# A window on the transfers in flight, a third Q/K buffer and a new plan for the attention stage

## Chip, cores, metric

One core of one Trainium2 chip. The metric is device time in microseconds of one execution.

## The reference

Sparse causal attention with a linear bias, then two blocks on its output. B = 2, H = 8, S = 768, D = 64, model width 512. All inputs are float32 but the weights, which arrive as float64.

```
scores = q @ k.T / sqrt(D) - slope[h] * dist          # keep: the last 96 keys, and the first 8
x = concat_heads(softmax(scores) @ v)                 # B x S x 512
u = x + ((x.T @ U @ V).T)                             # rank 32 over the sequence
x = u + relu(u @ w_ch1) @ w_ch2                       # 512 -> 2048 -> 512
xk, xr = mixes of x with x shifted by one row (mu_k, mu_r)
out = sigmoid(xr @ w_r) * (relu(xk @ w_k)**2 @ w_v)   # 512 -> 1024 -> 512
```

## The kernel before, in words

Attention goes by eight pairs of heads (`PRS`: two batches, four pairs each) and, in a pair, by six tiles of 128 queries. A tile's scores are products of `QS` with a window of 256 gathered columns of `KK` (`s_mm`, L446). VectorE adds the bias and takes the row minimum out of PSUM (`s_min`, L454), ScalarE takes exponentials (`s_exp`, L462), VectorE inverts the sums of three tiles (L467, L468), GpSimd scales (`s_norm`, L474). TensorE transposes the tile (`tp`, L481), ScalarE or VectorE copies it out (`PT`, L705 or L707), and TensorE multiplies with V (`p_first` L496, `p_rest` L507: "PV" here) into `xa` and `xb`, which go to `yp`.

Beside it, in the same stretch, run the constants `UV` and the first weight slices: a float64 tile of 512 KB comes in through the staging buffer `stg` (L687, three tiles; UV at L724) and is turned into a high and a low part by ScalarE (L641, L653), VectorE (L636, L645, L649) and GpSimd (L657): "a conversion". When the four pairs of the first batch are done, its rank-32 product follows: transposes `xtp` (L755) with evictions `xt`, `gps` (L773), the sums `gsum` and `uv` (L779 to L794), `hps` (L804) added to `yp` (L809), the split `us` (L840, L843), and 48 matmuls of the first slice of w_ch1, `aps` (L874). Then, from the transposes of the second batch on, the program is written out by hand: alternating blocks of 48 `aps` and 48 `bps` matmuls, then `kps`, `prs`, `pvs`.

What sets the order of all this up to the second batch's transposes is a planner, `Flow`. Every step (a few instructions) has a kind; `COST` gives the engine, how long it is held and how late its result is; `rank` plus `BIAS` order the steps that could start within `SLACK` of each other; `caps` hold the number of tiles of each pool. `Flow.run` picks a step, advances the engines' times and emits its instructions, so the order on every queue is fixed when the program is built. Loads are steps on SP (SyncE's queue, which issues the transfers in order): `dq` (Q, 384 KB), `dk` (K or V, 768 KB), `ds` (a staging tile, counted as 512 KB), `dm` (the constants `mu`). A load that needs a buffer stands behind the last step that reads the old tile. The pools: Q and K two tiles each (`qkp`), V two, P ten, PT eight.

The first pair's Q and K and the second's are issued before the planner begins. In SyncE's queue stands also the load of `flag_i` (L1117), which GpSimd computes; it decides whether a general path (not taken here) is run.

## Time and profile before

| | |
|---|---|
| median of 3 runs | 525.47 us (525.38 to 527.12) |
| the profiled execution's own time | 525.22 us |
| its span, first to last instruction | 523.4 us |
| TensorE busy | 503.3 us, 96% of the span |
| VectorE, ScalarE, GpSimd busy | 305.3, 217.0, 184.7 us |
| transfers on the hardware queue of SyncE | 46.28 MB in 13,248 packets |

The durations in the text are from the profiled execution. PE is TensorE's matmul, PEld its weight load, DVE is VectorE, ACT is ScalarE, POOL is GpSimd, SP is SyncE. A time in brackets behind a row is the idle time of the engine before it, with the instruction that ended it.

### The profile page before, as it was taken

The numbers are of one execution on the slowest core, as the hardware profiler recorded it, in microseconds if no ns is written. First come the engines' busy times: TensorE is split into PE (matmuls) and PEld (weight loads), VectorE is DVE, ScalarE is ACT, GpSimd is POOL, SyncE is SP. The second block draws the span as 40 slices with busy tenths as digits, with TensorE's granted clock in tenths as the row PEclk, the third lists the DMA queues.
The fourth block names the chain that finished last, engine by engine and source line by source line (L and its number), as shares of the span: only waits on it lengthen the run. The fifth ranks groups of instructions, "written<-read, shape, count | busy, mean of one in ns | idle before, by whom it ended". The sixth has DMA issues, their size and how long they took to land.

```text
span 523.4 us, 8648 instructions
## 1 busy us (share of the span) xinstructions
PE 503.3 (96%) x3314; PEld 411.2 (79%) x3314; DVE 305.3 (58%) x673; ACT 217.0 (41%) x507; POOL 184.7 (35%) x247
## 2 busy tenths in 40 slices
PE   7788999999999999999999999999999999999994
PEld 4577677778888888888888888887888888888884
DVE  6898997789983746528365837796043522352110
ACT  6798987535430503204032312444912441144100
POOL 7685786026400404004040403635712442144100
PEclk9999999999999999999999999999999999999998
DMA  8977542323451310403104310031001000100010
GB/s 316 352 285 264 199 153 83 121 81 106 150 194 34 103 58 10 152 0 111 51 13 149 122 40 0 20 142 41 0 21 40 22 0 21 41 20 1 21 41 27
DMA packets 13587, 47.19 MB, mean 90 GB/s; under 512 B 1760, under 2 KB 2144, under 8 KB 13536
## 3 DMA queue, kind: packets, MB, share of 16 engines
q1 hardware_dynamic: 13248, 46.28, 25.7%
q8 instruction: 28, 0.46, 0.3%
q10 hardware_dynamic: 288, 0.26, 0.2%
q14 instruction: 23, 0.19, 0.1%
HBM read 43.39 MB, written 3.15 MB: 89 GB/s over the span
## 4 chain that ended last, share of the span: by engine, by line
PE 79%; DVE 11%; DMA 4%; ACT 2%; issue 2%; POOL 0%; SPq 0%; DVEq 0%; ACTq 0%
PE aps L874 24%; PE bps L896 21%; PE pvs L1081 13%; PE kps L1051 10%; PE prs L1070 6%; DMA KK<-in_k_dram 3%; DVE cvc L645 2%; DVE P L454 2%; DVE cvc L649 2%; PE s L446 2%; DVE PT L707 1%; DMA stg<-in_wv_dram 1%; PE tp L481 1%; ACT P L462 1%; DVE yp L900 1%
## 5 line engine op out<-in xcount | busy, mean ns | idle before, releaser
L874 PE MATMUL aps<-us,w1s 128*128 128x512 f32 x576 | 133.5, 390 | 0.0
L896 PE MATMUL bps<-rs,w2s 128*128 128x512 f32 x576 | 132.5, 389 | 0.0
L896 PEld LDWEIGHTS bps<-rs,w2s 128*128 128x128 f32 x576 | 108.0, 188 | 23.3 <-PE gps L773 0.8
L874 PEld LDWEIGHTS aps<-us,w1s 128*128 128x128 f32 x576 | 107.8, 188 | 22.6 <-issue 0.4
L878 ACT ACTIVATE rs<-aps 128x512 fp32r<-128x512 f32 x48 | 28.2, 595 | 94.6 <-PE aps L874 94.5
L1051 PE MATMUL kps<-mix,wk 128*128 128x512 f32 x288 | 66.1, 389 | 0.5 <-ACT kf L1055 0.5
L1051 PEld LDWEIGHTS kps<-mix,wk 128*128 128x128 f32 x288 | 54.0, 188 | 12.1 <-ACT kf L1055 0.9
L1081 PE MATMUL pvs<-wv,kh 128*128 128x512 f32 (+1 forms) x208 | 61.9, 373 | 0.0
L882 DVE SCALAR_TENSOR_TENSOR rs<-aps,rs 128x512 fp32r<-128x512 f32 x48 | 32.7, 686 | 42.0 <-ACT rs L878 42.0
L645 DVE SCALAR_TENSOR_TENSOR cvc<-cvc,cvt 128x512 uint32<-128x512 uint32 (+1 forms) x53 | 50.8, 960 | 7.5 <-ACT cvc L641 6.2
L641 ACT ACTIVATE cvc<-stg 128x512 f32<-128x512 f32 (+1 forms) x53 | 35.1, 675 | 44.1 <-DMA stg<-in_w_dram 18.8
L900 DVE TENSOR_TENSOR yp<-bps,yp 128x512 f32<-128x512 f32 (+1 forms) x64 | 33.9, 550 | 25.7 <-PE bps L896 25.7
L474 POOL TENSOR_SCALAR P<-P,sm 128x192 f32<-128x192 f32 x96 | 43.4, 473 | 14.4 <-DVE sm L468 5.8
L1033 POOL TENSOR_SCALAR mixt<-yp,mu 128x512 f32<-128x512 f32 (+1 forms) x32 | 21.6, 681 | 74.2 <-DVE mixf L1035 29.6
L649 DVE SCALAR_TENSOR_TENSOR cvc<-stg,cvc 128x512 uint32<-128x512 uint32 x52 | 45.1, 874 | 0.6
L657 POOL TENSOR_TENSOR w2s<-cvc,w2s 128x512 fp32r<-128x512 f32 x16 | 23.2, 1466 | 62.9 <-ACT w2s L653 59.7
L657 POOL TENSOR_TENSOR w1s<-cvc,w1s 128x512 fp32r<-128x512 f32 x16 | 23.3, 1472 | 60.3 <-ACT w1s L653 59.7
L462 ACT ACTIVATE P<-P,nm 128x192 f32<-128x192 f32 x96 | 42.5, 448 | 3.0 <-DVE nm L454 2.7
L1081 PEld LDWEIGHTS pvs<-wv,kh 128*128 128x128 f32 x208 | 38.1, 188 | 6.9
L1061 POOL TENSOR_TENSOR kl<-kf,kh 128x512 fp32r<-128x512 f32 x24 | 31.0, 1292 | 30.6 <-ACT kh L1060 30.6
L1081 PE MATMUL pvs<-wv,kl 128*128 128x512 f32 (+1 forms) x104 | 38.8, 373 | 0.0
L1035 DVE SCALAR_TENSOR_TENSOR mixf<-yp,mu,mixt 128x512 f32<-128x512 f32 (+1 forms) x32 | 20.3, 653 | 29.8 <-POOL mixt L1033 29.7
(113 smaller groups left out, 586.9 us busy)
## 6 DMA issues: line engine op xcount, KB each, us to landing
stg<-in_w_dram SPq DMA_DIRECT2D x32, 512.0 KB, 4.0
vin<-in_v_dram SPq DMA_DIRECT2D x8, 768.0 KB, 5.2
KK<-in_k_dram SPq DMA_DIRECT2D x7, 768.0 KB, 7.2
stg<-in_wk_dram SPq DMA_DIRECT2D x8, 512.0 KB, 4.2
stg<-in_wv_dram SPq DMA_DIRECT2D x8, 512.0 KB, 3.6
out_dram<-sg SPq DMA_DIRECT2D x11, 256.0 KB, 2.0
QS<-in_q_dram SPq DMA_DIRECT2D x7, 384.0 KB, 5.6
stg<-in_wr_dram SPq DMA_DIRECT2D x4, 512.0 KB, 3.6
```

Source lines behind the costliest of these rows:

```text
L462: nc.scalar.activation(out=Px, in_=Px, func=ACTF.Exp, scale=-1.0, bias=z["nm"][:, i, x:x + 1], accum_out=z["sm"][:, i, x:x + 1])
L474: engine.tensor_scalar(out=Px, in0=Px, scalar1=z["sm"][:, i, x:x + 1], scalar2=1.0, op0=ALU.mult, op1=ALU.mult)
L641: nc.scalar.activation(out=z["c"].bitcast(F32), in_=parts(z)[1].bitcast(F32), func=ACTF.Copy, scale=2.0 ** -112)
L645: nc.vector.scalar_tensor_tensor(out=z["c"], in0=z["c"], scalar=3, in1=z["t"], op0=ALU.logical_shift_left, op1=ALU.bitwise_or)
L649: nc.vector.scalar_tensor_tensor(out=z["c"] if plain is None else plain, in0=parts(z)[1], scalar=0x80000000, in1=z["c"], op0=ALU.bitwise_a ...
L657: engine.tensor_tensor(out=lo, in0=z["c"].bitcast(F32), in1=hi.bitcast(F32), op=ALU.subtract)
L874: nc.tensor.matmul(rs[g, c, f], lhsT=wsl(("w1", g), lw, kk, f * 128, 128), rhs=us[c][:, lx, kk, :], start=(kk == 0 and n == 0), stop=(kk = ...
L882: nc.vector.scalar_tensor_tensor(out=r[:, 1, f, :], in0=rs[g, c, f], scalar=0.0, in1=r[:, 0, f, :].bitcast(F32), op0=ALU.max, op1=ALU.subt ...
L896: nc.tensor.matmul(ps, lhsT=wsl(("w2", g), lw, f, o * 128, 128), rhs=r[:, lx, f, :], start=(n == 0), stop=(n == 11))
L900: nc.vector.tensor_tensor(out=ys, in0=ps[:, a:e], in1=ys, op=ALU.add)
L1051: nc.tensor.matmul(ps, lhsT=wsl("wk", lw, kk, f * 128, 128), rhs=xk[:, lx, kk, :], start=(n == 0), stop=(n == 11))
L1081: nc.tensor.matmul(pv, lhsT=ks[c][lx][:, f, t * 128:(t + 1) * 128], rhs=wsl("wv", lw, f, c0, c1 - c0), start=(n == 0), stop=(n == 23))
```

## The change

- `Flow` keeps the list of transfers sent. `before(x)` goes back from transfer x and adds the planner's sizes until they pass `LIMIT`, 2,000 KB; the transfer found there must have landed before x is issued. The plan takes its end as a lower bound for x, and `link` writes the wait into the program (a dependency between the two transfers).
- Pools: Q and K three tiles each, P twelve, PT ten. The room comes from the descriptor scratch, which goes from its default to 1,024 bytes.
- V loads have a kind of their own (`dv`). `BIAS`, `SLACK`, `RATE`, `LAND` and the ranks of the conversions have other values, so that the planner comes to another order. The load functions return their instruction.

```diff
-        ... "ch": [("PE", 0.68, 0.95)], ...
+        ... "ch": [("PE", 0.68, 0.95, 0.15)], ...
-        "dq": [("SP", 0.45, 384.0)], "dk": [("SP", 0.45, 768.0)], "ds": [("SP", 0.45, 512.0)], "dm": [("SP", 0.45, 4.0)],
+        "dq": [("SP", 0.45, 384.0)], "dk": [("SP", 0.45, 768.0)], "dv": [("SP", 0.45, 768.0)], "ds": [("SP", 0.45, 512.0)], "dm": [("SP", 0.45, 4.0)],
-    BIAS = {"ch": -9, "vd": -36, "ttr": -1.5, "xt": -26, "y": 8, "hm": -14, "vps": -8, "ga": 11, "tp": 17, "pt": 1.1,
-            "exp": -21, "sm": -6}
+    BIAS = {"dv": 8, "va": -5, "pt": 2.3, "vps": -3, "vd": -14}
-    SWITCH, SLACK, RATE, LAND = 0.13, 0.06, 390.0, 2.1
+    SWITCH, SLACK, RATE, LAND, LIMIT = 0.13, 0.02, 380.0, 2.4, 2000
...
+    def before(self, x):
+        n = self.COST[x.kind][0][2]
+        for a in reversed(self.sent):
+            n += self.COST[a.kind][0][2]
+            if n > self.LIMIT:
+                return a
+        return None
...
+            first = self.before(x) if eng == "SP" else None
+            if first is not None:
+                go = max(go, first.end)
...
-            x.fn(eng) if len(self.COST[x.kind]) > 1 else x.fn()
+            x.ins = x.fn(eng) if len(self.COST[x.kind]) > 1 else x.fn()
+            if eng == "SP":
+                first = self.before(x)
+                if first is not None:
+                    self.link(x.ins, first.ins)
+                self.sent.append(x)
...
-            pt_p = pool("ptp", 8, "right", cctx)
+            pt_p = pool("ptp", 10, "right", cctx)
-            np_p = pool("npp", 10, "right", cctx)
+            np_p = pool("npp", 12, "right", cctx)
-            qk_p = pool("qkp", 2, "right", bctx)
+            qk_p = pool("qkp", 3, "right", bctx)
...
-                fl = Flow({"a": 4, "t": 4, "P": 10, "PT": 8, "q": 2, "k": 2, "v": 2, ...},
-                          {"PE": 5.9, "ACT": 6.6, "DVE": 6.4, "POOL": 10.0, "SP": 3.1}, 7.6)
+                fl = Flow({"a": 4, "t": 4, "P": 12, "PT": 10, "q": 3, "k": 3, "v": 2, ...},
+                          {"PE": 5.9, "ACT": 6.6, "DVE": 6.4, "POOL": 10.0, "SP": 3.1}, 10.0,
+                          lambda a, b: tc.add_manual_dep(a.ins, b.ins.name, mybir.DependencyInfo(
+                              mybir.DependencyClass.Sync, mybir.DependencyReason.DATA), reason="transfers"))
...
-                        def conversion(r, behind=None, shift=0):
+                        def conversion(r, behind=None, shift=0, early=0):
-                            ds = fl.add("ds", lambda: z.update(stage(src)), new=[toks["st"]], rank=r - 12, behind=[behind])
+                            ds = fl.add("ds", lambda: z.update(stage(src)) or z["dma"], new=[toks["st"]], rank=r - 12 + early, behind=[behind])
-                        uvd = conversion(24, lks[0])
-                        w1d = [conversion(r, lk, x) for r, lk, x in zip((34, 44, 54, 64), lks[1:], (-24, 0, 14, 9))]
+                        uvd = conversion(24, lks[0], 0, 0)
+                        w1d = [conversion(r, lk, *x) for r, lk, x in zip((34, 44, 54, 64), lks[1:], ((0, 0), (-1, 11),
+                                                                                       (0, -19), (18, 0)))]
                         for r in (84, 86, 88, 90):
-                            conversion(r)
+                            conversion(r, None, -5, 0)
...
-    nc = _bacc.Bacc("TRN2", target_bir_lowering=False, num_devices=1)
+    nc = _bacc.Bacc("TRN2", target_bir_lowering=False, num_devices=1, dynamic_dma_scratch_size=1024)
```

What this does to the order shows best in three places. In the changed program lines lie 17 to 20 lower down. SyncE's queue, from V of the first pair on (`QS`, `KK` and `vin` are tiles of Q, K and V, `stg` staging tiles; the numbers are tile numbers). Before:

```order
L342 DMA vin_211<-in_v_dram 128x1536
L219 DMA mu_59<-in_mu_dram 128x8
L687 DMA stg_214<-in_w2_dram 128x512
L687 DMA stg_216<-in_w2_dram 128x512
L687 DMA stg_218<-in_w2_dram 128x512
L1117 TENSOR_LOAD flag_i_62
L331 DMA QS_279<-in_q_dram 128x768
L337 DMA KK_289<-in_k_dram 128x1536
L342 DMA vin_293<-in_v_dram 128x1536
L331 DMA QS_352<-in_q_dram 128x768
L337 DMA KK_363<-in_k_dram 128x1536
```

Now:

```order
L359 DMA vin_211<-in_v_dram 128x1536
L348 DMA QS_213<-in_q_dram 128x768
L354 DMA KK_215<-in_k_dram 128x1536
L236 DMA mu_59<-in_mu_dram 128x8
L743 DMA stg_330<-in_UV_dram 128x384
L1137 TENSOR_LOAD flag_i_62
L348 DMA QS_352<-in_q_dram 128x768
L359 DMA vin_393<-in_v_dram 128x1536
L354 DMA KK_414<-in_k_dram 128x1536
L348 DMA QS_442<-in_q_dram 128x768
L706 DMA stg_505<-in_w1_dram 128x512
```

Q and K of the third pair (`QS_213`, `KK_215`) have moved ahead of the flag; the three w2 tiles are gone from here and UV has come forward.

ScalarE's queue where the rank-32 product of the first batch goes on after its transposes (`xt` evicted transposes, `P,sm` exponentials, `gsum` and `uv` the sums). Before, from the third instruction behind the last `xt` on:

```order
L705 COPY PT<-tp 128x384
L462 ACTIVATE P,sm<-P,nm 128x192 x6
L641 ACTIVATE cvc<-stg 128x512
L462 ACTIVATE P,sm<-P,nm 128x192 x5
L779 COPY gsum<-gps 32x512
L462 ACTIVATE P,sm<-P,nm 128x192
L653 CAST w1s<-cvc 128x512
```

Now:

```order
L724 COPY xt<-xtp 128x512 x5
L724 COPY PT<-tp 128x384
L479 ACTIVATE P,sm<-P,nm 128x192 x5
L798 COPY gsum<-gps 32x512
L672 CAST w1s<-cvc 128x512
L479 ACTIVATE P,sm<-P,nm 128x192 x3
```

Between the last `xt` and `gsum` there were 15 instructions (two exponentials and the four rows above `gsum`), and there are 6 now.

TensorE's queue at the end of the attention stage (`tp` transposes of P; the PV rows are left out). Before:

```order
L446 MATMUL s<-KK,QS 64x192 x8
L804 MATMUL hps<-uv 128x256 x2
L874 MATMUL aps<-us,w1s 128x512 x36
L481 MATMUL tp<-ident,P 128x128 x18
L755 MATMUL xtp<-ident,yp 128x128 x24
L773 MATMUL gps<-xt,uvf 32x512 x6
L896 MATMUL bps<-rs,w2s 128x512 x48
```

Now:

```order
L823 MATMUL hps<-uv 128x256 x2
L893 MATMUL aps<-us,w1s 128x512 x3
L498 MATMUL tp<-ident,P 128x128 x12
L893 MATMUL aps<-us,w1s 128x512 x33
L774 MATMUL xtp<-ident,yp 128x128 x24
L792 MATMUL gps<-xt,uvf 32x512 x6
L915 MATMUL bps<-rs,w2s 128x512 x48
```

The last PV stood behind `tp` x18 and directly ahead of `xtp`; now it stands behind `tp` x12, and 33 of the 48 `aps` matmuls have moved behind it. Between `gps` and the first `hps` of the first batch TensorE now has only 9 transposes, the scores of four tiles, one pair's PV and the scores of two tiles.

## Rows read from the trace of the kernel before

**Rows 1.** Busy time by stretch: PE, PEld, DVE, ACT, POOL, clock, DMA share, GB/s.

```profile
0.00:20.00 20.00, 13.41 (x164) 8.40 (x168) 14.34 (x80) 13.98 (x56) 15.37 (x57) 1.00 0.92 346
20.00:42.00 22.00, 19.38 (x459) 15.96 (x452) 18.73 (x93) 19.11 (x74) 15.65 (x36) 1.00 0.78 286
42.00:63.00 21.00, 20.49 (x386) 15.63 (x384) 20.50 (x83) 20.42 (x72) 12.40 (x25) 1.00 0.64 224
63.00:93.92 30.92, 28.74 (x424) 23.24 (x424) 25.37 (x67) 22.52 (x61) 23.06 (x33) 1.00 0.43 136
...
115.00:330.00 215.00, 215.00 (x951) 178.01 (x950) 135.43 (x204) 65.01 (x114) 54.02 (x40) 1.00 0.24 79
```

**Rows 2.** Timeline of PE: start us, us, what, [idle before <-releaser].

```profile
1.18 4.02 PE L362 MATMUL warm<-wz 128*128 128x512 bf16 x10 [1.18 <-DVE et L426]
...
7.30 1.53 PE L446 MATMUL s<-KK,QS 64*64 64x192 f32 x32 [1.08 <-DMA KK<-in_k_dram]
10.18 1.64 PE L446 MATMUL s<-KK,QS 64*64 64x192 f32 x32 [1.34 <-DMA KK<-in_k_dram]
...
19.43 1.53 PE L446 MATMUL s<-KK,QS 64*64 64x192 f32 x32 [1.43 <-DMA KK<-in_k_dram]
...
25.98 1.53 PE L446 MATMUL s<-KK,QS 64*64 64x192 f32 x32
...
40.12 1.23 PE L446 MATMUL s<-KK,QS 64*64 64x192 f32 x17 [2.09 <-issue]
...
54.78 1.92 PE L773 MATMUL gps<-xt,uvf 128*32 128x512 f32 x12
...
61.53 0.95 PE L446 MATMUL s<-KK,QS 64*64 64x192 f32 x16
...
67.20 0.73 PE L804 MATMUL hps<-uv 96*128 96x512 f32 x2
...
96.22 1.14 PE L755 MATMUL xtp<-ident,yp 128*128 128x128 f32 x8 [0.32 <-ACT xt L712]
```

**Rows 3.** Timeline of SyncE's queue: issues of V0, w2, K2 and K5.

```profile
3.06 0.45 SPq L342 DMA_DIRECT2D vin<-in_v_dram  x1
...
4.56 1.72 SPq L687 DMA_DIRECT2D stg<-in_w_dram  x3
...
11.58 0.43 SPq L337 DMA_DIRECT2D KK<-in_k_dram  x1
...
31.35 0.42 SPq L337 DMA_DIRECT2D KK<-in_k_dram  x1
```

**Rows 4.** Transfers, issue to landing: K2, K3, K5, V0, V2, third w2, UV.

```profile
KK<-in_k_dram SPq DMA_DIRECT2D x1, 768.0 KB, 7.7
KK<-in_k_dram SPq DMA_DIRECT2D x1, 768.0 KB, 10.2
KK<-in_k_dram SPq DMA_DIRECT2D x1, 768.0 KB, 7.0
vin<-in_v_dram SPq DMA_DIRECT2D x1, 768.0 KB, 8.9
vin<-in_v_dram SPq DMA_DIRECT2D x1, 768.0 KB, 4.3
stg<-in_w_dram SPq DMA_DIRECT2D x1, 512.0 KB, 10.1
stg<-in_UV_dram SPq DMA_DIRECT2D x1, 384.0 KB, 6.9
```

**Rows 5.** Timeline of DVE: its wait for UV.

```profile
39.93 0.36 DVE L636 TENSOR_SCALAR cvt<-stg 128x384 uint32<-128x384 uint32 x1 [1.09 <-DMA stg<-in_UV_dram]
```

**Rows 6.** Timeline of ACT: the last xt of the first batch, and gsum.

```profile
54.14 0.59 ACT L705 COPY xt<-xtp 128x512 f32<-128x512 f32 x1
...
61.52 0.56 ACT L779 COPY gsum<-gps 32x512 f32<-32x512 f32 x1
```

**Rows 7.** Groups of DVE up to 93.92 us: the longest step of a conversion.

```profile
L649 DVE SCALAR_TENSOR_TENSOR cvc<-stg,cvc 128x512 uint32<-128x512 uint32 x8 | 6.6, 829 | 0.1
```

More of the change, by code (lines that the diff above doesn't have):

```diff
@@ L71, with __init__ @@
         "rd": [("DVE", 0.57, 0.72)], "small": [("DVE", 0.10, 0.25)],
-        "dq": [("SP", 0.45, 384.0)], "dk": [("SP", 0.45, 768.0)], "ds": [("SP", 0.45, 512.0)], "dm": [("SP", 0.45, 4.0)],
+        "dq": [("SP", 0.45, 384.0)], "dk": [("SP", 0.45, 768.0)], "dv": [("SP", 0.45, 768.0)], "ds": [("SP", 0.45, 512.0)], "dm": [("SP", 0.45, 4.0)],
     }
-    BIAS = {"ch": -9, "vd": -36, "ttr": -1.5, "xt": -26, "y": 8, "hm": -14, "vps": -8, "ga": 11, "tp": 17, "pt": 1.1,
-            "exp": -21, "sm": -6}
+    BIAS = {"dv": 8, "va": -5, "pt": 2.3, "vps": -3, "vd": -14}
     MODE = {"s": 1, "pa": 2, "pb": 1, "hm": 3, "hn": 3}
     PORT = {("DVE", k) for k in ("cvt", "c2", "c3", "sm", "nm", "lo", "sl", "small")}
-    SWITCH, SLACK, RATE, LAND = 0.13, 0.06, 390.0, 2.1
-    def __init__(self, caps, now, queue):
+    SWITCH, SLACK, RATE, LAND, LIMIT = 0.13, 0.02, 380.0, 2.4, 2000
+    def __init__(self, caps, now, queue, link):
         self.caps, self.now, self.queue = caps, dict(now), queue
         self.steps, self.live, self.port = [], {p: [] for p in caps}, 0.0
+        self.sent, self.link = [], link
     def add(self, kind, fn, after=(), new=(), use=(), rank=0.0, behind=()):
@@ L218, in constants @@
         def constants():
-            nc.sync.dma_start(out=mu[:, 0:2, :], in_=mu_kr)
+            return nc.sync.dma_start(out=mu[:, 0:2, :], in_=mu_kr)
         def complement():
@@ L330, in load_q @@
                     st[pp]["QS"] = qk_p.tile([128, S], F32, tag="QS", name="QS")
-                eng.dma_start(out=st[pp]["QS"][:, c0:c1], in_=q[b, p, :, c0:c1])
+                return eng.dma_start(out=st[pp]["QS"][:, c0:c1], in_=q[b, p, :, c0:c1])
             def load_k(pp, c0=0, c1=KW, eng=nc.sync):
@@ L336, in load_k @@
                     st[pp]["KK"] = qk_p.tile([128, KW], F32, tag="KK", name="KK")
-                eng.dma_start(out=st[pp]["KK"][:, c0:c1], in_=k[b, p, :, c0:c1])
+                return eng.dma_start(out=st[pp]["KK"][:, c0:c1], in_=k[b, p, :, c0:c1])
             def load_v(pp):
@@ L341, in load_v @@
                 st[pp]["v"] = v_p.tile([128, NB, 2, D], F32, tag="vin", name="vin")
-                nc.sync.dma_start(out=st[pp]["v"].rearrange("p x t d -> p (x t d)"), in_=v[b, p])
+                return nc.sync.dma_start(out=st[pp]["v"].rearrange("p x t d -> p (x t d)"), in_=v[b, p])
             lims = limits(lambda dt, n, nm: st_p.tile([128, n], dt, tag="nm" if dt is I64 else "sm", name=nm))
@@ L532, in pairs @@
                             fl.live[t.pool].append(t)
-                    lv = fl.add("dk", lambda pp=pp: load_v(pp), new=[vt], rank=R - 4, behind=[lv, loads[pp + 1][2] if 0 < pp < NPR - 1 else None])
+                    lv = fl.add("dv", lambda pp=pp: load_v(pp), new=[vt], rank=R - 4, behind=[lv, loads[pp + 1][2] if 0 < pp < NPR - 1 else None])
                     e, P, PT, X, tp, o = {}, {}, {}, [Tok("t"), Tok("t")], {}, []
@@ L583, in attention_windows @@
                                              mybir.EngineType.Pool, mybir.EngineType.SP}):
-                fl = Flow({"a": 4, "t": 4, "P": 10, "PT": 8, "q": 2, "k": 2, "v": 2, "nm": 3, "sm": 3, "stg": 3, "cvt": 2,
+                fl = Flow({"a": 4, "t": 4, "P": 12, "PT": 10, "q": 3, "k": 3, "v": 2, "nm": 3, "sm": 3, "stg": 3, "cvt": 2,
                            "cvc": 4, "zt": ZT},
-                          {"PE": 5.9, "ACT": 6.6, "DVE": 6.4, "POOL": 10.0, "SP": 3.1}, 7.6)
+                          {"PE": 5.9, "ACT": 6.6, "DVE": 6.4, "POOL": 10.0, "SP": 3.1}, 10.0,
+                          lambda a, b: tc.add_manual_dep(a.ins, b.ins.name, mybir.DependencyInfo(
+                              mybir.DependencyClass.Sync, mybir.DependencyReason.DATA), reason="transfers"))
                 fl.taken("P", 7, 6.4)
@@ L664, in stage @@
                     z = {"st": stg_p.tile([128, 512], I64, tag="stg", name="stg")}
-                    src(z["st"])
+                    z["dma"] = src(z["st"])
                     return z
```

2 rows, old and new, of the table COST are left out of this document.

## The prediction

> **What bounds the kernel now.** I read the busy time by stretch first [rows 1]. From 115 to 330 us TensorE is busy for 215.00 of 215.00 us. The change moves nothing there; it moves the first 94 us, in which the planner interleaves attention with the first weights. Up to 93.92 us, where the first transpose of the second batch starts, TensorE is busy for 13.41 + 19.38 + 20.49 + 28.74 = 82.02 us, so it is idle for 11.90 us. Whatever part of those 11.90 us goes shortens the run one for one, as long as the same work stands behind it, and it does: the matmuls behind that point are the same in the same order. The clock column is 1.00 in all these stretches, so the clock has no part in the sum.
>
> Then I looked for what ends TensorE's idle times [rows 2]. It waits for K three times: 1.08 us for the rest of the first pair, 1.34 us for the second and 1.43 us for the third, whose scores start at 19.43. At 40.12 stand 2.09 us whose releaser the row does not name. The opening therefore hangs on transfers, and the issues and landings say why [rows 3, 4]. (Pairs are counted from 0 below: K2 is K of the third pair.) K2 is issued at 11.58 and lands 7.7 us later, at 19.3. Three things hold it: the two-deep buffer (scores of pair 0 end at 8.83), the load of the flag ahead of it in SyncE's queue, and three w2 transfers issued from 4.56 on.
>
> **The change part by part.**
>
> *Third Q/K buffer and the order of transfers.* The issue order puts Q and K of the third pair directly behind V0, ahead of the flag, and moves the w2 transfers far back. Where K then lands can be read from what took its place: V0 (issued 3.06) lands after 8.9 us, at 11.96, with 3,072 KB issued up to it; the third w2 tile (the last 0.57 us of the row at 4.56, so issued near 5.7) lands 10.1 us later, at 15.8, with 4,612 KB [rows 3, 4]. K2 now ends at 4,224 KB, hence near 14.8 us by the line through the two. TensorE's queue reaches those scores only after transposes and PV of pair 0, about where it did before (18.0, that is 19.43 less the wait). So the wait of 1.43 us goes and no more is sure: **-1.4 us**, between 0 (another input is late) and -3.0 (TensorE's idle 6.59 us up to 20 us, less the 1.18 us before its first matmul [rows 2] and the 1.08 and 1.34 us that nothing here moves).
>
> *The middle.* From 20 to 42 us TensorE is idle for 2.62 us [rows 1], 2.09 of it at 40.12, in front of the scores of pair 5. K of that pair had landed by then (issued 31.35, 7.0 us later [rows 3, 4]), so I can't put the gap down to K alone. In the same microseconds VectorE waited 1.09 us for UV [rows 5], which took 6.9 us [rows 4] and stood in the queue ahead of other work; UV now comes as the first staging tile: issued when V0 has landed, 11.96, and between V2's 4.3 and its own 6.9 us later [rows 4], so near 17 us. Bounds: 0, if the gap has a cause that stays, and -2.62. I take half, rounded up, since one of two possible causes is removed: **-1.4 us**.
>
> *The tail.* From 63 to 93.92 us TensorE is idle for 2.18 us [rows 1], and it waits 0.32 us more for an evicted transpose at 96.22 [rows 2]. Before, all 48 ch1 matmuls run ahead of the last pair's transposes and PV, so the pair's evictions are exposed at the end. Now 33 of them stand behind the last PV and cover evictions and the first copies of the second batch. I take two thirds: **-1.7 us** of -2.5, the rest kept because one more weight conversion than before falls behind the hps steps of the first batch (five, not four). The longest of its three VectorE steps is 0.83 us [rows 7], so it adds 2.5 us at most, and VectorE's idle time in that stretch, 5.55 us [rows 1], takes them.
>
> *The chain from gps to hps.* It gets less cover. Before, gps ends at 56.70 and hps starts at 67.20 [rows 2], 10.5 us, in which ScalarE reaches gsum only at 61.52 [rows 6], 15 instructions behind the last xt at 54.14. Now gsum is 6 instructions behind xt. The 15 take 6.9 us with their waits, 0.46 each, so nine fewer give 4.1 us and the chain takes 6.4. On TensorE stand, between gps and hps, the pieces that before ended at 62.48 [rows 2], 5.8 us. The wait is 0.6; with a little for slips **+0.8 us**, between 0 and 4.7 (the chain as long as before).
>
> *The window.* A transfer waits until it and all sent before it that are still on the way make up at most 2,000 KB. Counted in the planner's sizes UV (512) + mu + K2 + Q2 is 1,668, so UV waits for V0; K3 + V1 + Q3 is 1,920, so K3 waits for UV. Behind a waiting transfer stands everything in SyncE's queue, Q of the next pair first, and the scores wait for that. What it costs by rows: V alone, 768 KB, lands 4.3 us after its issue [rows 4]; at the 346 GB/s of the opening [rows 1] the bytes take 2.3 us, so 2.0 us are fixed. When K3 is released, V1 and Q3, 1,152 KB, are still on the way, 3.4 us of work for the DMA engines. That is more than 2.0, so they don't run dry: **0**. Bounds: -1 (shorter queues, earlier landings) and +3.1 (below).
>
> Against the window speaks the Trainium skill, "DMA: Bandwidth & Descriptors", section "Rules for kernel authors": issue a transfer early and wait for it late, so that its fixed cost lies beside work. The section on one DMA's anatomy fits 2.0 us plus bytes over 436 GB/s; by that rule K3, issued late, pays its fixed part on the path, an estimate of 2 us, and the sum below would be -1.7. The trace agrees on the fixed part, 2.0 us by the row of V alone; that a transfer held back pays it on the path, no row here shows.
>
> *More P and PT tiles, the smaller scratch, the new biases and costs of the planner.* No P or PT wait stands out before, and all transfers are issued by SyncE or ScalarE, so I price these at 0; if the scratch did matter, transfers would land late, which is the window's upper bound.
>
> **Sum:** -1.4 - 1.4 - 1.7 + 0.8 = -3.7 us. The profiled execution took 525.22 us, so 521.5; the median of the runs, 525.47, lies 0.25 us above it: **521.8 us**. About 0.5%, 2.6 us, is what a measurement of this kernel can tell from no change; the forecast lies 3.7 below.
>
> **The rivals.**
>
> *The chain gives it back.* TensorE waits the whole 4.7 us before hps. For it: from 42 to 63 us VectorE is busy for 20.50 of 21.00 and TensorE for 20.49 [rows 1], and a chain through both and ScalarE queues behind their work at each step, as it did before. Against it: nine instructions fewer ahead of gsum. Then -4.5 + 4.7 = +0.2, 525.7 us. Parts of it, 523 to 525.7, count here too: no change.
>
> *The window holds K back: slower.* UV waits for V0, K3 for UV. UV would be issued at 11.96 and, if it takes 6.9 us as before [rows 4], land at 18.9; K3 issued then and taking its old 10.2 us lands at 29.1, against scores that started at 25.98 [rows 2]. That is +3.1 us on a TensorE that has nothing else to do there, and it takes the place of the opening's and the middle's gain: 525.5 + 3.1 - 1.7 + 0.8 = 527.7 us, and 531.6 if the chain takes its 4.7 too. It decides from K3 landing later than about 24.5 us (25.98 less the opening's gain). Against it: 10.2 us was K3's time with a long queue ahead of it, which is what the window forbids; with 7.7 us [rows 4] and UV at 17 it lands at 24.7, just at the point.
>
> *It doesn't do what it says.* SyncE's queue is already held by buffers, so the window never ends last, and the new order merely moves waits: 525 us.
>
> *Everything goes.* Opening -3.0, middle -2.6, tail -2.5: 517.4 us. For it: every engine has idle time up to 94 us. Against it: new waits come with any new order.
>
> **How the numbers follow.** Forecast 0.50, with a range of its own from 519.5 to 523.5, of which 0.08 lies above 522.8 (525.5 less 0.5%). Chain 0.22, of which 0.04 below 522.8, 0.02 above 528.1 (0.5% more) and 0.16 between. Window 0.10, of which 0.06 above 528.1. Doesn't do what it says 0.04, no change. Everything goes 0.14. Faster: 0.42 + 0.04 + 0.14 = 0.60. Slower: 0.02 + 0.06 = 0.08. Within 0.5%: 0.32. The range leaves out about half of the best case and of the window's and the chain's upper ends: 517.9 to 525.9 us.
>
> **What would show it.** K2 landing by 15 us and its scores starting before 18.2 without a wait for K; no wait of VectorE for UV; TensorE's idle time up to the first transpose of the second batch about 8 us instead of 11.90; a wait of under 1.5 us in front of hps; the stretches behind the same to 0.2 us. The forecast is wrong if the wait before hps exceeds 3 us, or if scores of pairs 3 and 4 wait for K. It is right for the wrong reason if the time goes anywhere behind that point.

## The result and the profile after

The changed kernel took 520.52 us (median of 4 runs, 519.55 to 521.68), the kernel before 526.12 us (4 runs, 525.38 to 527.12): a ratio of 0.9897, 95% interval 0.987 to 0.9923. Run again beside the experiments it took 519.50 us (5 runs, 519.15 to 519.97), a ratio of 0.9878 (0.9858 to 0.9897). Forecast were 521.8 us (517.9 to 525.9) and a gain of 3.7; the gain is 5.6 us in the first comparison and 6.6 in the second.

The profiled execution of the changed kernel took 521.29 us, span 519.4 (before 525.22 and 523.4). Its busy time by stretch, up to the first transpose of the second batch, which now starts at 88.78 us (columns as in [rows 1]):

```profile
0.00:20.00 20.00, 16.33 (x248) 10.36 (x252) 15.25 (x92) 15.43 (x62) 15.04 (x58) 1.00 0.91 330
20.00:42.00 22.00, 20.12 (x425) 16.04 (x417) 20.74 (x94) 21.32 (x83) 16.02 (x36) 1.00 0.84 282
42.00:63.00 21.00, 19.96 (x375) 15.13 (x367) 20.54 (x81) 20.18 (x67) 14.05 (x29) 1.00 0.81 278
63.00:88.78 25.78, 25.45 (x399) 21.25 (x400) 21.86 (x59) 19.35 (x54) 18.55 (x26) 1.00 0.36 115
```

TensorE is idle for 3.67 + 1.88 + 1.04 + 0.33 = 6.92 us in place of 11.90, and the transpose starts 5.14 us earlier. The timeline of TensorE shows what went and what came:

```profile
7.67 1.15 PE L463 MATMUL s<-KK,QS 64*64 64x192 f32 x16 [0.17 <-PE s L463]
9.48 1.64 PE L463 MATMUL s<-KK,QS 64*64 64x192 f32 x32 [0.67 <-DVE nm L471]
...
14.88 0.55 PE L498 MATMUL tp<-ident,P 128*128 128x128 f32 x3 [1.33 <-POOL P L491]
...
17.02 1.53 PE L463 MATMUL s<-KK,QS 64*64 64x192 f32 x32
...
40.80 0.52 PE L498 MATMUL tp<-ident,P 128*128 128x128 f32 x3 [0.78 <-DVE PT L726]
...
58.35 0.27 PE L524 MATMUL xa<-PT,vin 64*64 64x64 f32 x2 [0.58 <-issue]
...
88.78 2.78 PE L774 MATMUL xtp<-ident,yp 128*128 128x128 f32 x24
...
106.68 1.16 PE L823 MATMUL hps<-uv 96*128 96x256 f32 x3 [1.32 <-DVE yp L919]
```

In this profile no score waits for K any more; those of the third pair start at 17.02, not 19.43 [rows 2]. The 2.09 us at 40.12 are gone, and no wait stands before the first hps (59.55 us). In their place stand short waits for VectorE and GpSimd. (The longest of them, 1.33 us for GpSimd at 14.88, is not new: before, TensorE waits for it 1.09 us at 15.32 and 0.26 us at 16.12.) SyncE's queue issues K of the third pair at 4.10 us, and it lands 10.1 us later, at 14.2 (before 11.58 and 19.3, [rows 3, 4]):

```profile
4.10 0.45 SPq L354 DMA_DIRECT2D KK<-in_k_dram  x1
...
11.32 0.33 SPq L743 DMA_DIRECT2D stg<-in_UV_dram  x1
```

```profile
KK<-in_k_dram SPq DMA_DIRECT2D x1, 768.0 KB, 10.1
```

Behind that point this execution gives some of it back. On VectorE a first conversion step (cvt) stands in front of the add for which TensorE waits 1.32 us, and itself waits for its weight tile:

```profile
105.60 0.43 DVE L655 TENSOR_SCALAR cvt<-stg 128x512 uint32<-128x512 uint32 x1 [1.60 <-DMA stg<-in_w_dram]
105.94 0.68 DVE L919 TENSOR_TENSOR yp<-bps,yp 128x512 f32<-128x512 f32 x1
```

Then the granted clock falls. In the second profile of the same kernel the wait is 1.06 us and the clock stays. By stretch (PE busy, clock, DMA share, GB/s), first profile and second:

```profile
108.00:112.00 4.00, 4.00 (x12) 0.57 0.00 0
```

```profile
108.00:112.00 4.00, 4.00 (x19) 1.00 0.00 0
```

From the first bps to the group of 90 aps it takes 16.79 us in the first profile, 15.45 in the second and 14.82 before; five aps take 2.23 us in the first and 1.32 in the second. The whole account of the first profile against before: -5.14 up to the transpose, -0.18 from it to the first bps, +1.97 up to the 90 aps, +0.46 up to the last pvs group, -1.08 behind its start: -4.0 us, the difference of the spans. The last term can't be put down to the change: from the issue of the last output to the end it takes 6.2, 6.2, 5.7 and 4.9 us in four profiles with the order of before (the kernel itself and the experiments with the tail, the scratch and the window alone).

### The profile page after: what moved, and what is told of

The parts are those of the page before. It is cut to its first block, busy times and chain, and to the rows that moved or that the text cites. A ratio compares the mean times of both kernels' runs of the same rounds, so it can differ in the third digit from the quotient of the medians.

```text
span 519.4 us, 8649 instructions
## 1 busy us (share of the span) xinstructions
PE 504.9 (97%) x3314; PEld 412.1 (79%) x3314; DVE 304.7 (59%) x672; ACT 217.7 (42%) x508; POOL 184.1 (35%) x247
## 3 DMA queue, kind: packets, MB, share of 16 engines
HBM read 43.39 MB, written 3.15 MB: 90 GB/s over the span
## 4 chain that ended last, share of the span: by engine, by line
PE 81%; DVE 11%; DMA 2%; ACT 2%; issue 1%; POOL 1%; POOLq 0%; SPq 0%; DVEq 0%; ACTq 0%
PE aps L893 26%; PE bps L915 19%; PE pvs L1101 13%; PE kps L1071 11%; PE prs L1090 6%; DVE P L471 3%; PE tp L498 2%; DVE cvc L664 2%; DVE cvc L668 2%; PE s L463 2%; DMA stg<-in_w_dram 1%; PE warm L379 1%; DMA stg<-in_wv_dram 1%; DVE yp L919 1%; PE xa L513 1%
## 5 line engine op out<-in xcount | busy, mean ns | idle before, releaser
L893 PE MATMUL aps<-us,w1s 128*128 128x512 f32 x576 | 135.3, 393 | 0.0
L664 DVE SCALAR_TENSOR_TENSOR cvc<-cvc,cvt 128x512 uint32<-128x512 uint32 (+1 forms) x53 | 48.6, 918 | 7.9 <-ACT cvc L660 6.4
L491 POOL TENSOR_SCALAR P<-P,sm 128x192 f32<-128x192 f32 x96 | 42.1, 461 | 16.5 <-DVE sm L485 9.6
```

What stands on the lines that cost most here:

```text
L491: engine.tensor_scalar(out=Px, in0=Px, scalar1=z["sm"][:, i, x:x + 1], scalar2=1.0, op0=ALU.mult, op1=ALU.mult)
L664: nc.vector.scalar_tensor_tensor(out=z["c"], in0=z["c"], scalar=3, in1=z["t"], op0=ALU.logical_shift_left, op1=ALU.bitwise_or)
L893: nc.tensor.matmul(rs[g, c, f], lhsT=wsl(("w1", g), lw, kk, f * 128, 128), rhs=us[c][:, lx, kk, :], start=(kk == 0 and n == 0), stop=(kk = ...
```

## The experiments

"First transpose" is that of the second batch, the milestone of the account above.

### The changed kernel once more

No edit.

> The changed kernel once more, unaltered. What it tells: whether the loss behind the stage belongs to the change. In its first profile TensorE waits 1.32 us at 105.36 us for a VectorE add, and from 108 to 112 us its granted clock is 0.50 to 0.66 (1.00 before the change). Theory 'by the order': the wait follows from the order on VectorE, so it stands here again with 1.0 to 1.6 us at about 105 us, the clock falls behind it again, and the span is 519 to 520 us. Rival 'chance of one execution': no wait over 0.6 us there or no fall of the clock, and a span near 517.7 us. The first transpose of the second batch at 88.8 us in either case.

519.50 us; first transpose at 89.35; the wait at 105.4 is 1.06 us, the clock stays at 1.00 (row above). So the wait belongs to the order, the fall of the clock to some executions. The five runs agree with that: their mean clock is 0.998 to 0.999.

### No window

```diff
-  lambda a, b: tc.add_manual_dep(a.ins, b.ins.name, ..., reason="transfers")
+  lambda a, b: None
```

> The changed kernel with the same order of instructions, but no transfer waits for transfers sent before it (its buffers alone hold it). Theory 'the window is worth 0', as the prediction had it: K of the third pair lands between 14 and 15.5 us, no score waits over 0.5 us for K, the first transpose of the second batch stands at 88.8 us to 0.4, and the time is that of the changed kernel to 0.6 us. Rival 'the window brings K forward': without it UV, V1 and K3 share the DMA engines with K2, K2 and K3 land 2 us later or more, TensorE waits 1 to 3 us for K up to 30 us, the transpose stands at 90 to 92 us, and the time is 1.2 to 3 us above the changed kernel's. Rival 'the window pays its fixed cost on the path': without it the transpose stands before 87.5 us and the time is 1.3 to 2 us below.

520.49 us (6 runs, 519.5 to 521.97), 0.99 above the changed kernel beside it (519.15 to 519.97); first transpose at 89.75, against 88.78 and 89.35 with the window. The loss of 1 us is likely, not certain: the ranges touch, the intervals of the two ratios to the kernel before overlap (0.9874 to 0.9914 here, 0.9858 to 0.9897 with the window), and in the first comparison the changed kernel itself had 0.9897, the ratio here being 0.9894. K of the third pair lands at 14.6 (issued 4.42, 10.2 us), K of the fourth at 21.3 (12.19, 9.2 us), as in the first profile with the window; one score waits 0.94 us for K, that of the second pair at 9.99. So neither theory of K holds, and the time is between the first two. What did come back are gaps without a named releaser, on TensorE's timeline:

```profile
38.41 0.27 PE L524 MATMUL xa<-PT,vin 64*64 64x64 f32 x2 [0.64 <-issue]
...
46.03 0.33 PE L513 MATMUL xb<-PT,vin 128*64 128x64 f32 x2 [1.36 <-issue]
```

These are two gaps of the kind that stood at 40.12 before the change [rows 2], in another order. Ahead of each a packet of the DMA queue that the page calls "instruction" (16 KB each) had landed 1.3 us earlier, at 37.11 and 44.76. Before the change such a packet ran from 37.64 to 38.62:

```profile
q8 instruction: 1, 0.02, 5.5%
```

That is the row of the DMA view of the kernel before from 37.6 to 38.7 us (queue, packets, MB, share). From here on there was a new theory: TensorE ran out of instructions, because their packet stood behind the transfers.

### 24 small matmuls more at the start

The kernel before with these behind the ten warm-up matmuls:

```diff
+  for _ in range(24):
+      nc.tensor.matmul(wps[0:32, 0:32], lhsT=wz[:, 0:32], rhs=wz[:, 0:32], start=True, stop=True)
```

> The kernel before with 24 small matmuls more (32x32, of zeros) behind the ten warm-up matmuls, nothing else. It is about the 2.09 us at 40.12 us, whose releaser is not named. They cut a group of 32 score matmuls in two (15 of them run before the gap), 626 weight loads and their like into TensorE's program, and a packet of the instruction queue lands 1.5 us before TensorE goes on (37.64 to 38.62 us). Theory 'TensorE runs out of instructions': the place is counted in instructions, so the gap moves 24 matmuls forward in the program, to the PV matmuls of the pair before (L509 here), again near the 626th record, with 0.5 to 2.5 us and a packet of the instruction queue ending 1.2 to 1.6 us ahead of its end. Rival 'the scores wait for K or UV': the gap stays in front of or inside the scores of pair 5. Time: that of the kernel before to 1.5 us (the small matmuls fall mostly into the wait for the rest of K of the first pair, 1.08 us).

The gap moved exactly as the first theory says: out of the scores, into the middle of a PV group, 24 matmuls earlier in the program. It ends 1.35 us behind a packet that landed at 38.15.

```profile
39.50 0.36 PE L509 MATMUL xb<-PT,vin 64*64 64x64 f32 x1 [2.46 <-issue]
```

The expectation of the time was wrong: 529.01 us, a ratio of 1.0069 (1.0048 to 1.009). The clock falls behind the gap (two rows by stretch, columns as above), and again behind a wait of 1.51 us at 52.58:

```profile
38.00:40.00 2.00, 0.50 (x13) 0.88 0.02 3
40.00:42.00 2.00, 2.00 (x29) 0.50 0.49 134
```

Counted in the trace (weight loads and the other records of TensorE's sequencer), 626 records precede this gap, the gap before the change and the first gap without a window; the second one comes 132 records later. The place is a count, not a wait for data, in two different orders. The soonest packets start within 0.1 us of the 246th and of the 502nd record and 0.23 us behind the 374th, 128 apart; taking these as the moments when packets are due, this is the one due at the 502nd (us):

```
kernel                       due    starts  landed  goes on  gap
before                       34.08  37.64   38.62   40.12    2.09
tail alone                   33.89  37.72   38.70   40.05    2.21
scratch alone                33.97  36.90   37.85   39.38    1.47
window alone                 33.99  36.71   37.64   39.13    1.19
24 small matmuls more        31.76  37.22   38.15   39.50    2.46
change without window        32.80  36.18   37.11   38.41    0.64
change, window 2,600 KB      32.43  36.34   37.28   38.59    1.19
change, first profile        32.48  35.06   36.01   -        0
change, second profile       33.03  34.21   35.23   -        0
change, conversion moved     32.76  33.27   34.26   -        0
change, old tail             32.54  33.07   34.09   -        0
change, window 1,300 KB      38.26  38.24   39.30   -        0
change, two buffers          33.46  36.61   37.56   -        0
buffers alone                31.27  37.32   38.29   -        0
```

In every gap TensorE goes on 1.3 to 1.5 us after the landing. In the changed order the packet starts when it is due with 1,300 KB at most on the way, 0.5 to 2.6 us late with 2,000 (3.2 with two buffers, where the loads come in another order), and 3.4 and 3.9 us late without a window and with 2,600; the gap stands only in the last two. In the order of before it starts 2.7 to 5.5 us late, with a gap each time. Late alone is not enough for a gap, TensorE has to reach the 626th record first: with the buffers alone the packet starts 6.0 us late and nothing stands there, since TensorE, held up by other waits, comes to that record only at 41.05. The window does not always suffice: the 0.58 us at 58.35 in the first profile of the change is such a gap, behind a packet that ran from 55.99 to 56.96.

The Trainium skill, "Runtime: NRT & Kernel Launch", section "Instruction fetch mechanics", says that an engine gets its instructions in blocks of 16 KiB or 256 instructions over a DMA queue, the next one while it works on the current one, and that the cost is mostly hidden. The trace agrees on the block (one 16 KB packet for 128 weight loads with their matmuls) and not on the cost: it is 0.6 to 2.5 us in the gaps of this table, with a DMA share of 0.85 to 0.98 from the moment when those packets are due to their landing.

### The window alone

The kernel before with the window from V of the third pair on.

```diff
+  if first is not None and len(self.sent) >= 10:
+      self.link(x.ins, first.ins)
```

> The kernel before, order and buffers unaltered, with the window of 2,000 KB from V of the third pair on (issued at 22.75 us; the opening is left as it was). It is the window alone where the gap of 2.09 us stands. Theory 'TensorE runs out of instructions because their packet queues behind the transfers': fewer kilobytes are on their way at 34 us (UV waits for V, 34.4 us, in place of 32.99), so the packet that started at 37.64 us starts before 37, the gap falls to 1.5 us or less, and the time falls by 0.5 to 2 us. Rival 'the gap has another cause': it stays at 1.8 to 2.3 us, and the time is the same to 0.6 us. Rival 'the waits cost': scores of pairs 4 to 6 wait for K, and the time rises by 1 us or more.

523.29 us (12 runs) against 524.93: a ratio of 0.9977 (0.9957 to 0.9998). The packet starts at 36.71 and the gap is 1.19 us; a second one of 0.55 us stands at 46.40.

```profile
39.13 1.23 PE L461 MATMUL s<-KK,QS 64*64 64x192 f32 x17 [1.19 <-issue]
...
46.40 0.27 PE L522 MATMUL xa<-PT,vin 64*64 64x64 f32 x2 [0.55 <-issue]
```

These are the three signs of the first theory, but the profiles don't carry it: the one with the scratch alone has no window, and its packet starts at 36.90 with a gap of 1.47 us (table above). The idle time is no better either (11.34 us up to the first transpose against 10.49 there). The median gains 1.6 us nevertheless, with an interval that ends just below 1. The clock is a part of it at most. Runs with a lower mean clock are slower (of 71 runs of the kernel before that were made beside these experiments, 10 have 0.998 and take 524.6 us on average, 13 have 0.994 and take 526.7), and 8 of the 12 with the window alone have 0.997 or more, against 11 of the 23 beside them. But at 0.998 the four runs with the window take 522.9 us on average and the five of the kernel before beside them 524.5. Where the rest comes from is open.

### A tighter and a looser window

The changed kernel, its order kept, with 1,300 and with 2,600 KB:

```diff
-  first = self.before(x)
+  first = self.before(x, 1300)
```

> The changed kernel with the same order of instructions, but transfers wait until at most 1,300 KB are on their way in place of 2,000. Theory 'the window is there for TensorE's instruction packets': from 30 to 60 us those packets start sooner after they are due (in the changed kernel 1.2 to 4.9 us later, without a window up to 5.1), no gap without a named releaser stands, and what is lost is lost to K or V: with K of the fourth pair issued when less is on the way, scores wait 0.5 to 3 us for K or V somewhere between 20 and 60 us, and the time is 0.5 to 4 us above the changed kernel's 519.5. Rival 'a tighter window is better still': no new wait for K or V over 0.4 us, time 518.5 to 519.5 us.

533.87 us, 14.4 above the changed kernel: the direction of the first theory and several times its price. The instruction packets now start within 2 us of being due up to 70 us, and K is late:

```profile
28.76 2.84 PE L463 MATMUL s<-KK,QS 64*64 64x192 f32 x32 [3.91 <-DMA KK<-in_k_dram]
...
42.01 1.53 PE L463 MATMUL s<-KK,QS 64*64 64x192 f32 x32 [2.45 <-DMA KK<-in_k_dram]
...
52.37 2.15 PE L498 MATMUL tp<-ident,P 128*128 128x128 f32 x9 [4.95 <-ACT yp L724]
```

> The changed kernel with the same order of instructions, but transfers wait until at most 2,600 KB are on their way in place of 2,000: a point between the change (median 519.5 us) and no window (520.5 us). Theory 'the window keeps the queue ahead of TensorE's instruction packets short, and 2,000 KB is enough for the rest': the packets due at the 502nd and 630th record start later than in the changed kernel (1.2 to 2.6 us after they are due), 2.6 to 5 us, part of the gap that stands without a window comes back (0.3 to 1.5 us), and the time is 519.5 to 520.6 us. Rival 'a looser window loses less to K and V': no gap without a named releaser, K earlier, and the time is 518.5 to 519.4 us.

520.45 us (519.39 to 521.46), the time without a window. The packet due at the 502nd record starts 3.9 us late, and 1.19 us come back, as the first theory says:

```profile
38.59 0.27 PE L524 MATMUL xa<-PT,vin 64*64 64x64 f32 x2 [1.19 <-issue]
```

Of 1,300, 2,000, 2,600 KB and no window, 2,000 KB has the lowest median: 14 us below the tighter one, which is clear, and about 1 us below the looser ones, which is not (ratio 0.9902, 0.9873 to 0.9931, with 2,600 KB; 0.9878, 0.9858 to 0.9897, with 2,000).

### Two buffers for Q and K in the new order

```diff
-  qk_p = pool("qkp", 3, "right", bctx)
+  qk_p = pool("qkp", 2, "right", bctx)
```

> The changed kernel with the same order on TensorE, VectorE, ScalarE and GpSimd, but two buffers for Q and K in place of three (the load of the flag moves ahead of Q of the third pair in SyncE's queue). Theory 'the third buffer carries the opening': K of the third pair can't be issued before the scores of the first pair end (near 8.5 us; now 4.1 us), lands at 15.5 us or later (now 14.2), the later K's each come later too, TensorE's idle time up to 20 us is 5 us or more (now 3.67), and the first transpose of the second batch stands 1.4 to 3 us later than 88.8 us. Rival 'the order alone carries it': K of the third pair is in time for its scores at 17.0 us either way, the transpose stands at 88.8 to 89.3 us, and the time is that of the changed kernel to 0.6 us.

529.44 us, slower than before the change (1.0057, 1.0035 to 1.008), first transpose at 97.72. In the opening the first theory holds: K of the third pair is issued at 11.73, TensorE is idle for 5.04 us up to 20 us, with this wait:

```profile
18.01 1.53 PE L463 MATMUL s<-KK,QS 64*64 64x192 f32 x32 [1.11 <-DMA KK<-in_k_dram]
...
48.61 0.34 PE L513 MATMUL xa<-PT,vin 128*64 128x64 f32 x4 [3.95 <-DMA vin<-in_v_dram]
```

But most is lost later, which neither theory foresaw. SyncE's queue holds Q of the seventh pair until a buffer is free (40.15), and V of the fourth stands behind it: it is issued at 41.00 us in place of 34.93 and lands 7.5 us later. The PV that needs it waits 3.95 us, and the clock falls to its lower level, 1.2 GHz:

```profile
50.00:52.00 2.00, 1.51 (x28) 0.50 0.89 345
```

### The buffers alone

The kernel before with the three numbers for the buffers and the scratch; the old biases, no window; the planner orders anew.

```diff
-  fl = Flow({"a": 4, "t": 4, "P": 10, "PT": 8, "q": 2, "k": 2, ...
+  fl = Flow({"a": 4, "t": 4, "P": 12, "PT": 10, "q": 3, "k": 3, ...
```

> The kernel before with the buffers of the change alone: three for Q and K, 12 and 10 for P and PT, the smaller scratch; no window, the planner's old biases and costs. The planner's order moves with the buffers: Q and K of the third and fourth pair are issued one behind the other, UV comes before the w2 tiles, V of the second pair behind both, 36 ch1 matmuls stay ahead of the last pair's PV. Theory 'the third buffer carries the opening, the biases and the window the rest': no wait for K over 0.5 us up to 30 us, idle time of TensorE up to 20 us 3.5 to 5 us (before 6.59), a gap whose releaser is not named stays somewhere from 30 to 50 us, and the time is 1.5 to 4 us below the kernel before. Rival 'the buffers bring nothing without the order': within 1 us of the kernel before, or slower.

526.57 us, slower than before (1.0035, 1.001 to 1.0059). The opening is the best of all, and its gain is lost behind it (PE busy, clock, DMA share, GB/s; up to the first transpose):

```profile
0.00:20.00 20.00, 16.85 (x214) 1.00 0.94 356
20.00:42.00 22.00, 19.34 (x414) 1.00 0.84 311
42.00:63.00 21.00, 19.16 (x394) 1.00 0.58 203
63.00:96.60 33.60, 29.58 (x424) 0.95 0.34 112
```

Idle time is 3.15 us in the opening (before 6.59), but 1.84 from 42 to 63 us (0.51) and 4.02 in the tail (2.18), where the last transposes wait 1.35 and 1.46 us for evictions, at 89.53 and 91.87, and the clock is 0.95. A gap without a named releaser stands too, 0.42 us at 31.24. So the opening's gain comes with the third buffer, and in the order that the planner finds with the old biases it is lost again.

### The old tail in the new kernel, and the new tail in the old

```diff
+  tail = [x for x in fl.steps if x.kind == "tp"][-4:]
+  tail[0].behind.append([x for x in fl.steps if x.kind == "ch"][-1])
```

> The changed kernel with the old tail: the last four transposes of the last pair and its PV stand behind all 48 ch1 matmuls, as before the change, and everything ahead of them is as in the changed kernel. Theory 'the 33 matmuls behind the last PV cover the evictions': TensorE waits again before the first transposes of the second batch, they start 1.2 to 2.2 us later than 88.8 to 89.4 us, and the time is 1.2 to 2.2 us above the changed kernel's (519.5 us in the same batch of runs). Rival 'the tail was no part of the gain': the time is the changed kernel's to 0.5 us, and what the stretch from 63 us on lost (2.18 us of idle time to 0.3) came from hps and scores placed differently ahead of it.

521.23 us, 1.73 above the changed kernel (by the ratios to the kernel before, 0.9926 and 0.9878, 2.5); the first transpose at 91.25, 1.9 later than in its second profile, and the wait for an evicted transpose is back:

```profile
85.04 2.56 PE L895 MATMUL aps<-us,w1s 128*128 128x512 f32 x10 [0.88 <-POOL w1s L678]
...
91.25 2.20 PE L776 MATMUL xtp<-ident,yp 128*128 128x128 f32 x16
93.76 1.14 PE L776 MATMUL xtp<-ident,yp 128*128 128x128 f32 x8 [0.31 <-ACT xt L733]
```

Only part of that speaks for the first theory. 0.5 us of the 1.9 stand ahead of the moved instructions, in the same order as in the changed kernel: TensorE waits 1.07 us for K of the seventh pair at 47.21. From the last hps ahead of the moved instructions (77.36) to the first bps (97.12) it takes 19.76 us, against 17.50 in both profiles of the changed kernel. Of these 2.3 us, 0.88 are a wait for a converted weight tile, `w1s`, which the matmuls reach sooner in this order, and 0.31 the wait for the evicted transpose; behind the stage the wait for the add is 0.43 us again and not 1.06.

```diff
-  BIAS = {"ch": -9, "vd": -36, ...
+  BIAS = {"ch": 0, "vd": -36, ...
```

> The kernel before with the tail alone: of the 48 ch1 matmuls ahead of the last pair's transposes, 33 now stand between and beside those transposes (three or more behind each), all still ahead of its PV; everything up to there as before. Theory 'matmuls behind the transposes cover the evictions': TensorE's idle time from 63 us to the first transpose of the second batch falls from 2.18 to 1 us or less, that transpose starts 0.8 to 2 us earlier against the matmuls of 63 us, and the time is 0.8 to 2 us below the kernel before. Rival 'it is the place behind the last PV that counts' (the copies of the last PV's result stay uncovered here): 1.5 us or more of the idle time stay, and the time is the same to 0.6 us.

525.13 us against 525.53: the runs show no difference (0.9968 to 1.0011), and don't rule out the 0.8 us of the first theory. The profile speaks for it by the measure that it named, the stretch up to the first transpose. Before, TensorE waits inside the last PV for an evicted tile of that pair (second row; the first is the longest other wait of this stretch, for GpSimd):

```profile
63.84 1.50 PE L481 MATMUL tp<-ident,P 128*128 128x128 f32 x12 [0.88 <-POOL P L474]
...
91.63 0.34 PE L496 MATMUL xb<-PT,vin 128*64 128x64 f32 x4 [0.86 <-DVE PT L707]
```

With the tail alone the second wait is gone, and from the first hps (68.26) to the first transpose (93.98) it takes 25.7 us, against 26.7 before (67.20 to 93.92 [rows 2]) and also 26.7 with the scratch alone and with the window alone. The first transpose stands no earlier because this execution lost as much ahead of the first hps, where the clock fell behind the gap of 2.21 us at 40.05. By stretch, that fall and the tail:

```profile
42.00:44.00 2.00, 2.00 (x12) 0.50 0.98 364
...
63.00:93.98 30.98, 29.53 (x441) 1.00 0.44 137
```

The idle time of the tail, 30.98 - 29.53 = 1.45 us (before 2.18), stays above the 1 us expected; 0.84 us of it are a wait for GpSimd at 64.91. A wait of 0.30 us for an evicted transpose of the second batch also stays, at 96.26; in the changed kernel it is gone.

Together: matmuls beside the last pair's transposes cover the eviction of its tiles, 1.0 us in the profile, and those behind its PV also the copies of its result. What each is worth in the median the runs don't show.

### The smaller scratch alone

```diff
-  nc = _bacc.Bacc("TRN2", target_bir_lowering=False, num_devices=1)
+  nc = _bacc.Bacc("TRN2", target_bir_lowering=False, num_devices=1, dynamic_dma_scratch_size=1024)
```

> The kernel before with the smaller descriptor scratch alone. Theory 'the scratch is worth 0': all transfers go through SyncE's and ScalarE's queues, issues and landings stand where they stood, the first transpose of the second batch at 93.9 us to 0.5, and the time is that of the kernel before to 0.6 us. Rival 'it matters': landings in the opening change by 1 us or more, and the time by 0.8 us or more.

525.64 us against 525.53 (ratio 0.998 to 1.0038): no difference. The first transpose at 93.17 is 0.75 us earlier than in the profile before, more than the 0.5 expected; the gap in front of the scores is 1.47 us there and not 2.09 (table above). So much do two profiles of one order differ.

### The conversion step behind the add

```diff
+  if z.get("n") == 6 and last_yp[0]:
+      tc.add_manual_dep(x.ins, last_yp[0].ins.name, ..., reason="behind")
```

> The changed kernel with one instruction moved: on VectorE the first conversion step (cvt) of the sixth weight tile behind the stage, which there waits 1.60 us for its tile's transfer at 105.6 us, goes behind the add of the last bps group, for which TensorE waits 1.32 us. Theory 'the wait and the clock behind it are the give-back': TensorE's wait at 105.4 us falls to 0.5 us or less, the clock stays at 1.00 from 108 to 112 us (at 0.50 to 0.66 over 4 us it cost about 1.7 us), and the time is 1.5 to 2.6 us below the changed kernel's. Rival 'the clock falls without the wait': the wait goes, the clock falls nevertheless, and the time is 0.4 to 1.0 us below. Rival 'the wait moves on': the conversions that now come later hold up the next matmuls, and the time is the changed kernel's to 0.4 us.

519.07 us (5 runs, 518.69 to 519.79), 0.43 below the changed kernel. The wait is what it was before the change, and the clock stays at 1.00:

```profile
106.06 1.16 PE L828 MATMUL hps<-uv 96*128 96x256 f32 x3 [0.43 <-DVE yp L924]
```

The 1.5 us expected were wrong, since the changed kernel's own clock does not fall in most runs; what is left to win is the wait, 1.06 - 0.43 = 0.63 us. It has the lowest median of all, but the runs of the two overlap, so that it beats the changed kernel isn't shown.

## Why the prediction was right, and where it was not

**Opening** (forecast -1.4, bounds 0 and -3.0). Idle time up to 20 us went from 6.59 to 3.67, -2.9. The mechanism was right: K of the third pair landed at 14.2 (forecast 14.8) and its scores no longer wait; two buffers bring a wait of 1.11 us back. The step that failed is "the 1.08 and 1.34 us that nothing here moves": in the changed kernel 0.17 and 0.67 us stand there, for other scores and VectorE. Part of that is chance: in three more profiles with the old opening the idle time is 6.27, 6.01 and 5.49 us, 6.1 on average with the first, so that 2.4 us belong to the change.

**Middle** (forecast -1.4, about half of 2.62). Idle time fell by 0.74, from 2.62 to 1.88. The step that failed is the cause: "one of two possible causes is removed". The gap was neither K's nor UV's; TensorE waited for instructions. The 2.09 us went whole, and 1.82 us of short waits for VectorE and GpSimd (0.65, 0.39 and 0.78 in the second profile) stand in the stretch instead. The order alone doesn't remove such gaps: without the window 0.64 us stand at the same record and 1.36 at the next packet's. So the forecast was nearly twice too large, and right in its sign by luck. UV did land in time, and VectorE no longer waits for it; what that is worth was not tried by itself.

**Tail** (forecast -1.7 of -2.5). -1.85 in idle time. The reason, the last pair's evictions, holds for 0.86 us of it (the wait at 91.63), and for the 0.32 us at 96.22, which are gone too. The largest wait of the stretch before, 0.88 us at 63.84, is for GpSimd's scaling, which the 33 matmuls can't cover; it went with the rest of the new order, and that the number is so close is luck. Undoing the tail costs 1.73 us of the median, in the profile about 0.9 us of it by a wait for weights.

**Chain** (forecast +0.8). 0, since hps does not wait. The cover was counted rightly: in the second profile TensorE works for 5.80 us from the end of gps to hps, and in the first 6.6 us pass (52.97 to 59.55), the gap of 0.58 us at 58.35 included. The step that failed is the length of the chain, 6.4 us: the last piece of uv is there 5.4 us after gps in both profiles (58.40 and 58.96).

**Window** (forecast 0, bounds -1 and +3.1). About -1 by the run without it, at the lower bound and hardly clear of the spread. The argument for 0 (that the DMA engines don't run dry) held for K of the third and fourth pair, which landed at about the same time either way; it left out the one other customer of the queues. Later K's do land later with the window, that of the seventh pair at 44.8 to 47.0 and not at 41.2, and in one profile (old tail) its scores wait 1.07 us. The rival in which the window holds K back is what happens at 1,300 KB. By the rule of the Trainium skill ("DMA: Bandwidth & Descriptors", "Rules for kernel authors") to issue early and wait late, the run without the window should have gained about 2 us; it lost one. The 2.0 us of fixed time in that argument are shown by no row. They were read from V of the third pair as if it went alone, but K of the fourth pair was still on the way when that V was issued at 22.75 (issued 13.82, landed 10.2 us later [rows 4]), and the fit in the Trainium skill's section on one DMA's anatomy is for transfers that GpSimd issues, while these go through SyncE's queue:

```profile
13.82 0.43 SPq L337 DMA_DIRECT2D KK<-in_k_dram  x1
22.75 0.33 SPq L342 DMA_DIRECT2D vin<-in_v_dram  x1
```

**42 to 63 us** (no term of the sum). Idle time rose from 0.51 to 1.04 us in the first profile, by the gap of 0.58 us at 58.35; in the second it is 0.62.

**Behind the stage** (forecast "the same to 0.2 us"). Wrong by the wait for the add, 1.06 to 1.32 us in place of 0.43, and in one profile of two by the clock.

The sum of the idle times, 4.98 us, is 1.3 more than the 3.7 forecast. That the medians gained 5.6 and 6.6 fits the clock of the kernel before, which falls in more of its runs than that of the changed one (beside each other 14 runs have 0.992 to 0.998, and five 0.998 to 0.999); in the prediction's sum the clock had no part, since in the one profile at hand it was 1.00. Where the mean clock is 0.998 on both sides, the kernel before takes 524.6 us on average (10 runs) and the changed one 520.1 (4 of its 9 runs), 4.5 less, which is near the idle time. That the first profile's own account, -4.0 us, comes so near the forecast of -3.7 is luck: 5.3 us gained up to the first bps, 2.4 lost behind it and 1.1 gained at the end, for which nothing in the change stands.

## What to carry to other kernels

A stall whose releaser the profile doesn't name, in the middle of a group of like instructions, may be the engine's own instruction packet behind data transfers: look for a packet of the instruction queue that lands just before it goes on, and shift the program by a few instructions to see whether the stall keeps its count or its place. A limit on what is on the way at once can then pay, as long as it lets through what the next step needs: 2,000 KB gained about 1 us here, hardly clear of the spread, and 1,300 lost 14. A third buffer, a new order and a window that lean on one another should be undone one at a time before any of them is credited: here the buffer without the order and the order without the buffer were both slower than the old kernel.

## What the runs showed that was not expected

Instruction packets compete with data: the one due at the 502nd record started when it was due with 1,300 KB at most on the way, and up to 6.0 us late where nothing limited the transfers. The clock falls to 0.50 for some microseconds behind some stalls of TensorE and not behind others: it did behind 2.46 and 2.21 us of idle time, and behind 1.32 and 1.27 us at 106 us (the latter without a window), but not behind 2.09 us in the profile before, 1.06 us at the same place or 1.33 us in the opening. What decides was not settled. And the stretch from the last output's issue to the end of the program varies by over a microsecond between executions of one order.
